# When a weight is converted: fewer conversion steps ahead of the last two layers, earlier low parts, a subtraction in two halves

## The chip, the cores and the metric

The kernel runs on one core of a Trainium2 chip. The core has TensorE (PE in the rows; its weight loads are PEld), VectorE (DVE), ScalarE (ACT), GpSimd (POOL) and SyncE (SP), which here only issues transfers. Each engine works through a queue of its own, strictly in order, and waits at an instruction until what it reads or overwrites is free. The metric is the device time of one execution in microseconds (us).

## The reference, cut to what matters

Three blocks in a row: attention with pooled keys and values (4 x 8 heads, 576 positions), a mixture of 8 experts over its 2304 tokens of 512 numbers, and a dense pair of layers. The change lies in the last one:

```
h = x @ w_in              # x: tokens x 512, w_in: 512 x 2048
r = np.maximum(h, 0.0)
g = s * (r * r) + b
return (g @ w_out)        # w_out: 2048 x 512
```

The weights w_in and w_out come as 64-bit floats. Tokens that an expert had no room for are zero at this point and all give the same row.

## The kernel before

**Numbers as high and low parts.** TensorE is given every operand twice: a high part (the value rounded by a cast, `w1h`, `yhl`, `gh`) and a low part (the value less the high part, `w1l`, `y1l`, `gl`). A product is three matmuls: high x high, high x low, low x high.

**The last layers** (`last_layers`) take the kept tokens in units of 256 (`CU`). Layer 1 makes the 2048 hidden numbers in 16 blocks `f` of 128 (`KF2`); one block is 12 matmuls of 256 columns (`layer1_y`, line 1040) into one PSUM bank. The block is then squared (`square`): ACT writes relu to `rt` (line 1424), DVE multiplies (line 1425); ACT casts the result to the high part `gh` (`parts`, line 1439) and POOL subtracts to get the low part `gl` (line 1440). Of every third block (`inside`, `f % 3 == 2`) DVE leaves the square in the PSUM bank and makes the low part itself; that bank is free only after this. Layer 2 is 6 matmuls of 512 columns per block (`layer2`, line 1445): two halves of the tokens, three products each.

**w_out.** It is loaded by SP in 16 pieces of 128 rows (line 1471) and rebuilt from its 64-bit pattern by `Weights64.step`: four steps a piece, each one or two DVE instructions (lines 871 to 883). The step after next then makes the high part (ACT, line 1399; for the first three pieces POOL, line 1397) and the low part (DVE, line 1400), and one adds the piece to a sum of rows in `raw3` (DVE, line 1405). `conv(n, end)` issues the next n steps. All this stands in the DVE queue between the squares.

**Units 0 and 1 go as a pair** (`pair`), because w_out isn't ready when they begin: layer 1 of unit 0, all 16 blocks (`first(0, 0, 16)`; the first four of them, `EARLY`, were multiplied at the end of the experts); layer 1 of unit 1, blocks 0 to 6 (`HEAD` = 7); layer 2 of both units for blocks 0 to 6 (`second`); layer 1 of unit 1, blocks 7 to 15; layer 2 of both for blocks 7 to 15. Unit 0's first layer goes round 8 PSUM banks, unit 1's round 4 (`ph`), while the other 4 (`po`) hold the sums of layer 2. Pieces 14 and 15 of w_out are loaded only after the first part of layer 2, into space that held parts of unit 1 till then. The tokens of unit 1 (`yr`) are loaded by SP behind piece 5; their high and low parts (`split_y`: ACT line 1032, DVE line 1033) are needed by unit 1's first block.

**Then come single units** (`unit`, four of them here), with POOL and DVE as above and nothing of w_out left to convert, **and at the end a unit of 128 tokens** (`half`): its first layer uses the sum of w_in's two parts as a single-precision weight, which DVE and POOL rebuild by turns, three blocks ahead (`whole`, line 1557), and its `gl` subtractions (128 columns) are POOL's as well.

The order is written out by hand: each engine's queue is the order of the calls below.

Of the kernel before, what the change touches and what calls it, by code (L numbers as in the profile page):

```python
# [33 lines left out]
KD = DM // P  # L34
# [541 lines left out]
HEAD = 7  # L576
# [793 lines left out]
def last_layers(nc, tc, c, a, pool, side, x, ps, out):  # L1370
# [13 lines left out]
    FIRST = len(x.c_raw)  # L1384
# [29 lines left out]
    def conv(n, end=len(steps)):  # L1414
        for _ in range(n):
            if done[0] < end:
                z, i = steps[done[0]]
                z.step(i)
                done[0] += 1

    def square(f, p, n, inside=False):

        r = rt[f % 4][:, :n]
        nc.scalar.activation(r, p, AF.Relu)  # L1424
        nc.vector.scalar_tensor_tensor(out=p if inside else r, in0=p, scalar=0.0, in1=r, op0=ALU.max, op1=ALU.mult)  # L1425

    def place(f, u=0):

        if u != 1 or HEAD <= f < KF2 - 2:
            f -= HEAD if u == 1 else 0  # L1430
            return gh[:, f], gl[:, f]
        t = spare[f % (KF2 - 2)] if f < 3 or f > HEAD else more[(f - 3) // 2][:, (f - 3) % 2]
        return t[:, 0], t[:, 1]

    def parts(f, n=CU, u=0, p=None):

        h, l = place(f, u)
        r = rt[f % 4][:, :n] if p is None else p
        nc.scalar.copy(h[:, :n], r)  # L1439
        (nc.gpsimd if p is None else nc.vector).tensor_sub(l[:, :n], r, h[:, :n])  # L1440

    def layer2(p, j, f, c=slice(0, DM), u=0):
        h, l = place(f, u)
        for i, (g, z) in enumerate(((h, 0), (h, 1), (l, 0))):
            nc.tensor.matmul(p[:, c], lhsT=g[:, j * P:j * P + P], rhs=wo[f][:, z, c], start=f == 0 and i == 0, stop=f == KF2 - 1 and i == 2)  # L1445
# [12 lines left out]
    def tokens(u):  # L1458
        if u < NV:
            for k in range(KD):  # L1460
                x.split_y(u, k, nc.gpsimd)
# [8 lines left out]
    def load_out(i):  # L1470
        nc.sync.dma_start(out=wo[i].rearrange("p c two -> p (c two)"), in_=wout[:, i])

    def pair():

        for i in range(KF2 - 2):
            load_out(i)
            if i == 5:
                x.load_y(1)
                for j, n in enumerate(("moe2_s", "moe2_b")):
                    nc.sync.dma_start(out=sb[:, j:j + 1], in_=a[n].unsqueeze(0).to_broadcast([P, 1]))  # L1480
        more.extend(side.tile([P, 2, 2, CU], F32R, name=f"wo{i}") for i in range(KF2 - 2, KF2))
        spare.extend(x.w.tile([P, 2, CU], F32R, name=f"raw{i}") for i in range(3))
        held = []

        def first(u, f0, f1, banks):
            for n, f in enumerate(range(f0, f1)):
                p = banks[f % len(banks)][:, :CU]
                if u or f >= EARLY:
                    x.layer1_y(u, p, *win[f])
                inside = f % 3 == 2  # L1490
                square(f, p, CU, inside)
                conv(1, steps_of_first)
                if u == 0 and 10 <= f < 10 + KD:
                    x.split_y(1, f - 10, nc.vector)
                if held:
                    parts(*held.pop())
                held.append((f, CU, u, p if inside else None))
            parts(*held.pop())

        def second(u, f0, f1, end):  # L1500
            for f in range(f0, f1):
                for j in range(2):
                    layer2(po[2 * u + j], j, f, u=u)
                conv(2, end)

        steps_of_first, all_steps = cvs[0].total, len(steps)
        conv(4 * FIRST)
        nc.gpsimd.memset(onesf, 1.0)
        first(0, 0, KF2, ps)
        first(1, 0, HEAD, ph)  # L1510
        x.load_y(2)
        second(0, 0, HEAD, steps_of_first)
        second(1, 0, HEAD, steps_of_first)
        for i in range(KF2 - 2, KF2):
            wo[i] = place_out(i, [P, DM, 2], I32)
            load_out(i)
        first(1, HEAD, KF2, ph)
        conv(all_steps, steps_of_first)
        second(0, HEAD, KF2, all_steps)
        tokens(2)  # L1520
        second(1, HEAD, KF2, all_steps)
        conv(all_steps)
        raw[0:3] = [x.w.tile([P, DM], F32, name=f"raw{i}") for i in range(3)]
        slots.extend(raw[2:4] + [x.w.tile([P, DM], F32, name="c_f1")])
        sums["drop"] = x.w.tile([P, DM], F32, name="c_u0")

    def unit(u):
        if u == 2:
            pair()
        if u + 1 < NV:  # L1530
            x.load_y(u + 1)
        for f in range(KF2):
            p = ph[f % 4][:, :CU]
            x.layer1_y(u, p, *win[f])
            square(f, p, CU)
            if f:
                parts(f - 1)
            if u == 2:
                if f == 1:
                    rows(ph[(f + 3) % 4])  # L1540
                elif f > 11:
                    store((f - 12) // 2, f % 2, po[f - 12])
        parts(KF2 - 1)
        tokens(u + 1)
        if u == 2:
            for f in range(len(slots)):
                whole(f)
        for j in range(2):
            p = po[2 * (u % 2) + j]
            for f in range(KF2):  # L1550
                layer2(p, j, f)
            store(u, j, p)
# [95 lines left out]
```

## Time and profile before

| | us |
|---|---|
| median of 3 runs | 648.42 (647.5 to 651.75) |
| the profiled execution | 649.79 |
| its span in the trace | 648.1 |
| PE busy | 588.7 (91%) |
| DVE busy | 367.0 (57%) |
| POOL busy | 267.8 (41%) |
| granted TensorE clock, mean | 0.959 |

The trace is of one execution; its times count from the start of the span, and the 1.7 us between span and execution lie around it. The last layers take from about 324 us to the end: the pair to 427 us, four single units to about 606 us, the half unit after that. A row of a timeline merges instructions of one kind that follow each other; in brackets stands how long the engine sat idle before, and what ended that.

### The profile page before, as it was taken

What the parts mean: (1) busy time and instruction counts of PE and PEld (TensorE: products, weight loads), DVE (VectorE), ACT (ScalarE), POOL (GpSimd) and SP (SyncE); (2) the same over time, 40 slices, a digit from 0 to 9 for tenths busy, and PEclk for the clock granted to TensorE, in tenths of its full rate; (3) what the DMA queues carried; (4) which work ended last, traced back from release to release, by engine and by line L of the source; (5) the groups of instructions that cost most, each with busy time, mean ns of one, the idle gap of its engine ahead of it and who ended that gap; (6) DMA issues with size and microseconds to landing.
All of it is one profiled execution on the core that took longest, in us unless ns stands there. A gap on an engine that the chain in (4) does not pass through costs nothing. (4 is left out here: it accounts for less than half of the span.)

```text
span 648.1 us, 11186 instructions
## 1 busy us (share of the span) xinstructions
PE 588.7 (91%) x4005; PEld 545.1 (84%) x4005; DVE 367.0 (57%) x893; ACT 249.9 (39%) x614; POOL 267.8 (41%) x384
## 2 busy tenths in 40 slices
PE   5887988799899979998887899999999999999894
PEld 5787877689799969997887889899899898898784
DVE  4687898888969956654499996424122021120140
ACT  1354554546356635533327425125034042141130
POOL 6557634627165717013234402216435054153381
PEclk8799999799899979999998799999999999999898
DMA  8999776637649884856565101135200101000000
GB/s 164 190 190 182 157 228 182 220 117 261 230 148 307 267 299 126 281 172 214 188 208 231 34 30 37 32 118 209 81 18 6 46 17 33 32 3 17 20 2 20
DMA packets 67950, 86.11 MB, mean 133 GB/s; under 512 B 24713, under 2 KB 40073, under 8 KB 67856
## 3 DMA queue, kind: packets, MB, share of 16 engines
q1 hardware_dynamic: 57168, 71.04, 37.2%
q10 hardware_dynamic: 8240, 7.14, 3.8%
q0 software_dynamic: 2448, 6.82, 3.3%
q8 instruction: 42, 0.69, 0.5%
q14 instruction: 52, 0.43, 0.2%
HBM read 68.09 MB, written 17.58 MB: 132 GB/s over the span
## 5 line engine op out<-in xcount | busy, mean ns | idle before, releaser
L1440 POOL TENSOR_TENSOR gl<-rt,gh 128x256 fp32r<-128x256 f32 (+1 forms) x96 | 71.3, 747 | 99.3 <-ACT gh L1439 57.9
L1445 PE MATMUL bank<-wo,gh 128*128 128x512 f32 (+1 forms) x340 | 99.2, 376 | 0.0
L1113 PE MATMUL bank<-hs,w2h 128*128 128x288 f32 (+1 forms) x308 | 68.9, 312 | 5.0 <-issue 4.6
L936 POOL TENSOR_TENSOR w1l<-kraw,w1h 128x128 fp32r<-128x128 f32 x96 | 51.9, 572 | 51.1 <-ACT w1h L929 51.1
L1445 PEld LDWEIGHTS bank<-wo,gh 128*128 128x128 f32 x340 | 62.0, 188 | 12.2
L1445 PE MATMUL bank<-wo,gl 128*128 128x512 f32 (+1 forms) x170 | 63.8, 375 | 0.0
L1452 DVE SCALAR_TENSOR_TENSOR raw<-bank,sb,c_u 128x512 f32<-128x512 f32 (+1 forms) x14 | 9.9, 710 | 86.9 <-PE bank L1445 86.9
L1113 PEld LDWEIGHTS bank<-hs,w2h 128*128 128x128 f32 x308 | 51.0, 193 | 6.0 <-issue 5.4
L1424 ACT ACTIVATE rt<-tq 128x256 f32<-128x256 f32 (+1 forms) x26 | 9.5, 367 | 113.8 <-PE tq L1040 91.1
L1113 PE MATMUL bank<-hs,w2l 128*128 128x288 f32 (+1 forms) x148 | 45.0, 304 | 0.0
L1425 DVE SCALAR_TENSOR_TENSOR rt<-bank,rt 128x256 f32<-128x256 f32 (+1 forms) x53 | 21.3, 401 | 37.6 <-ACT rt L1424 37.2
L944 POOL DMA_INDIRECT xg<-xd,u_idx x23 | 26.1, 1136 | 34.4 <-DVE r L290 15.3
L1439 ACT CAST gh<-rt 128x256 fp32r<-128x256 f32 (+1 forms) x96 | 36.6, 381 | 7.9 <-DVE rt L1425 7.9
L1453 POOL DMA_INDIRECT out_dram<-raw,it x12 | 11.9, 994 | 64.3 <-DVE raw L1452 63.8
L1445 PEld LDWEIGHTS bank<-wo,gl 128*128 128x128 f32 x170 | 31.9, 188 | 6.5
L1424 ACT ACTIVATE rt<-bank 128x256 f32<-128x256 f32 (+1 forms) x60 | 22.2, 369 | 33.7 <-PE bank L1040 26.5
L230 PE MATMUL sc<-kbd,qT 128*128 128x144 f32 (+1 forms) x152 | 25.5, 317 | 6.2 <-DVE rmine L380 3.6
L1425 DVE SCALAR_TENSOR_TENSOR rt<-tq,rt 128x256 f32<-128x256 f32 (+1 forms) x24 | 9.6, 399 | 35.5 <-ACT rt L1424 35.5
L967 PE MATMUL bank<-xs,w1h 128*128 128x288 f32 (+1 forms) x120 | 27.3, 313 | 2.0 <-DVE hs L970 2.0
L230 PEld LDWEIGHTS sc<-kbd,qT 128*128 128x128 f32 (+1 forms) x152 | 21.9, 201 | 8.4 <-issue 4.9
L1113 PEld LDWEIGHTS bank<-hs,w2l 128*128 128x128 f32 x148 | 28.5, 193 | 0.0
L940 DVE TENSOR_TENSOR w2l<-vraw,w2h 128x512 fp32r<-128x512 f32 x39 | 26.8, 686 | 0.9 <-ACT w2h L939 0.5
(496 smaller groups left out, 1749.4 us busy)
## 6 DMA issues: line engine op xcount, KB each, us to landing
kraw<-in_moe_w_dram SPq DMA_DIRECT2D x14, 1024.0 KB
vraw<-in_moe_w_dram SPq DMA_DIRECT2D x14, 1024.0 KB
c_raw<-in_moe_w_in_dram ACTq DMA_DIRECT2D x13, 512.0 KB
wo<-in_moe_w_out_dram SPq DMA_DIRECT2D x13, 512.0 KB
kraw<-in_k_dram SPq DMA_DIRECT2D x8, 576.0 KB
out_dram<-c_u SPq DMA_DIRECT2D x1, 4608.0 KB
q<-in_q_dram SPq DMA_DIRECT2D x16, 256.0 KB
xd<-xr SPq DMA_DIRECT2D x16, 256.0 KB
```

The lines of the kernel that those rows point to most:

```text
L230: nc.tensor.matmul(sc[:n, p // 2, p % 2 * 144:p % 2 * 144 + 144], lhsT=q[:, p, :n], rhs=kbd[b % 2][:, p], start=True, stop=True)
L936: eng.tensor_sub(self.w1l[:, i, z], self.w1(i)[:, z], self.w1h[:, i, z])
L940: eng.tensor_sub(self.w2l[i], self.w2r[:, i], self.w2h[i])
L944: self.nc.gpsimd.indirect_dma_start(out=dst, out_offset=None, in_=self.xd[:have], in_offset=bass.IndirectOffsetOnAxis(ap=idx[:n], axis=0), ...
L967: self.nc.tensor.matmul(p, lhsT=l[:, f, k], rhs=r[k], start=n == 0, stop=n == 3 * KD - 1)
L1113: nc.tensor.matmul(py[d][:, :v.n], lhsT=l[f][:, d * P:d * P + P], rhs=r[f], start=f == 0 and i == 0, stop=f == KF - 1 and i == 2)
L1424: nc.scalar.activation(r, p, AF.Relu)
L1425: nc.vector.scalar_tensor_tensor(out=p if inside else r, in0=p, scalar=0.0, in1=r, op0=ALU.max, op1=ALU.mult)
L1439: nc.scalar.copy(h[:, :n], r)
L1440: (nc.gpsimd if p is None else nc.vector).tensor_sub(l[:, :n], r, h[:, :n])
L1445: nc.tensor.matmul(p[:, c], lhsT=g[:, j * P:j * P + P], rhs=wo[f][:, z, c], start=f == 0 and i == 0, stop=f == KF2 - 1 and i == 2)
L1453: i = nc.gpsimd.indirect_dma_start(out=dst, out_offset=bass.IndirectOffsetOnAxis(ap=ids, axis=0), in_=o[:, c], in_offset=None, bounds_chec ...
```

## The change

Four edits in the last layers. (1) Ahead of the first square 6 conversion steps are issued instead of 12 (`conv(2 * FIRST)`), in unit 0's blocks 6 to 15 only every second block issues one, and the steps left over follow later: one instead of two after each block of unit 1's first part of layer 2, and one or two in each of unit 1's blocks 7 to 15, which had none. (2) Unit 1's tokens are split at blocks 7 to 10 of unit 0 instead of 10 to 13. (3) `conv(all_steps, steps_of_first)` ahead of the second part of layer 2 goes, since nothing is left for it. (4) POOL's `gl` subtraction is issued as two halves, in every unit.

```diff
         h, l = place(f, u)
         r = rt[f % 4][:, :n] if p is None else p
         nc.scalar.copy(h[:, :n], r)
-        (nc.gpsimd if p is None else nc.vector).tensor_sub(l[:, :n], r, h[:, :n])
+        if p is None:
+            for z in (slice(0, n // 2), slice(n // 2, n)):
+                nc.gpsimd.tensor_sub(l[:, z], r[:, z], h[:, z])
+        else:
+            nc.vector.tensor_sub(l[:, :n], r, h[:, :n])
...
                 square(f, p, CU, inside)
-                conv(1, steps_of_first)
-                if u == 0 and 10 <= f < 10 + KD:
-                    x.split_y(1, f - 10, nc.vector)
+                conv(f < 6 or f % 2 if u == 0 else 1 if f < HEAD else 1 + f % 2, steps_of_first)
+                if u == 0 and 7 <= f < 7 + KD:
+                    x.split_y(1, f - 7, nc.vector)
...
                     layer2(po[2 * u + j], j, f, u=u)
-                conv(2, end)
+                conv(1 if u and f < HEAD else 2, end)
...
         steps_of_first, all_steps = cvs[0].total, len(steps)
-        conv(4 * FIRST)
+        conv(2 * FIRST)
...
         first(1, HEAD, KF2, ph)
-        conv(all_steps, steps_of_first)
         second(0, HEAD, KF2, all_steps)
```

DVE's queue where unit 0's squares begin (`c_f`: a piece being rebuilt, `c_raw2` and `wo3`: raw pieces 2 and 3, `rt` and `bank2 <- ...`: squares of blocks 0, 1, 2). Before:

```order
L1400 TENSOR_TENSOR c_raw1_17124<-c_f1_17064,c_raw1_17124 128x512
L879 SCALAR_TENSOR_TENSOR c_f0_17063<-c_raw2_17081,c_f0_17063 128x512
L1405 TENSOR_TENSOR raw3_1963<-raw3_1963,c_f1_17064 128x512
L883 SCALAR_TENSOR_TENSOR c_f0_17063<-c_u0_17065,c_f0_17063 128x512
L1425 SCALAR_TENSOR_TENSOR rt0_1968<-tq_1607,rt0_1968 128x256
L871 TENSOR_SCALAR c_f1_17064<-wo3_17080 128x512
L1425 SCALAR_TENSOR_TENSOR rt1_1969<-misc_1608,rt1_1969 128x256
```

and now, from the square of block 3 on:

```order
L871 TENSOR_SCALAR c_f0_17063<-c_raw2_17081 128x512
L1425 SCALAR_TENSOR_TENSOR rt3_1971<-bank3_1943,rt3_1971 128x256
L874 TENSOR_SCALAR c_u0_17065<-c_raw2_17081 128x512
L877 SCALAR_TENSOR_TENSOR c_f0_17063<-c_raw2_17081,c_f0_17063 128x512
L1400 TENSOR_TENSOR c_raw1_17139<-c_f1_17064,c_raw1_17139 128x512
L1444 TENSOR_TENSOR gl_17067<-bank2_1942,gh_17066 128x256
```

Piece 2 was finished ahead of the square of block 0; now four squares have gone by when its first step is issued, and piece 1's low part comes behind the square of block 3.

DVE's queue where unit 1's blocks 7 to 15 begin (`rt3 <- bank3` is block 7's square, `tq <- tq` block 8's). Before:

```order
L1400 TENSOR_TENSOR wo13_17632<-c_f1_17064,wo13_17632 128x512
L1405 TENSOR_TENSOR raw3_1963<-raw3_1963,c_f1_17064 128x512
L1425 SCALAR_TENSOR_TENSOR rt3_1971<-bank3_1943,rt3_1971 128x256
L1425 SCALAR_TENSOR_TENSOR tq_1607<-tq_1607,rt0_1968 128x256
L1425 SCALAR_TENSOR_TENSOR rt1_1969<-misc_1608,rt1_1969 128x256
L1440 TENSOR_TENSOR gl_17067<-tq_1607,gh_17066 128x256
L1425 SCALAR_TENSOR_TENSOR rt2_1970<-bank2_1942,rt2_1970 128x256
```

and now:

```order
L871 TENSOR_SCALAR c_f1_17064<-wo11_17072 128x512
L1425 SCALAR_TENSOR_TENSOR rt3_1971<-bank3_1943,rt3_1971 128x256
L877 SCALAR_TENSOR_TENSOR c_f1_17064<-wo11_17072,c_f1_17064 128x512
L1400 TENSOR_TENSOR wo10_17654<-c_f0_17063,wo10_17654 128x512
L879 SCALAR_TENSOR_TENSOR c_f1_17064<-wo11_17072,c_f1_17064 128x512
L1405 TENSOR_TENSOR raw3_1963<-raw3_1963,c_f0_17063 128x512
L1425 SCALAR_TENSOR_TENSOR tq_1607<-tq_1607,rt0_1968 128x256
L883 SCALAR_TENSOR_TENSOR c_f1_17064<-c_u0_17065,c_f1_17064 128x512
L1425 SCALAR_TENSOR_TENSOR rt1_1969<-misc_1608,rt1_1969 128x256
L871 TENSOR_SCALAR c_f0_17063<-wo12_17071 128x512
L877 SCALAR_TENSOR_TENSOR c_f0_17063<-wo12_17071,c_f0_17063 128x512
L1400 TENSOR_TENSOR wo11_17694<-c_f1_17064,wo11_17694 128x512
```

All 14 pieces of the first load stood converted ahead of block 7's square; now piece 11 has just been begun there, and 14 steps stand among the nine squares.

POOL's queue in the half unit (`raw`, `c_f`: rebuilt single-precision weights). Before:

```order
L1557 TENSOR_TENSOR raw2_17932<-w2h0_146,w2l0_147 128x512
L1440 TENSOR_TENSOR gl_17067<-rt1_1969,gh_17066 128x128
L1440 TENSOR_TENSOR gl_17067<-rt2_1970,gh_17066 128x128
L1557 TENSOR_TENSOR c_f1_17933<-w2h_1951,w2l_1952 128x512
L1440 TENSOR_TENSOR gl_17067<-rt3_1971,gh_17066 128x128
```

and now:

```order
L1560 TENSOR_TENSOR raw2_17954<-w2h0_146,w2l0_147 128x512
L1442 TENSOR_TENSOR gl_17067<-rt1_1969,gh_17066 128x64 x2
L1442 TENSOR_TENSOR gl_17067<-rt2_1970,gh_17066 128x64 x2
L1560 TENSOR_TENSOR c_f1_17955<-w2h_1951,w2l_1952 128x512
L1442 TENSOR_TENSOR gl_17067<-rt3_1971,gh_17066 128x64 x2
```

Between two weights that POOL rebuilds stand four subtractions of 64 columns instead of two of 128.

## Rows read from the trace of the kernel before

**Rows 1.** Page, part 1: engine, busy us (share of the span), instructions.

```profile
PE 588.7 (91%) x4005; PEld 545.1 (84%) x4005; DVE 367.0 (57%) x893; ACT 249.9 (39%) x614; POOL 267.8 (41%) x384
```

**Rows 2.** Windows of 5 us: busy PE, PEld, DVE, ACT, POOL; granted clock, DMA share, GB/s.

```profile
335.00:340.00 5.00, 3.42 (x27) 3.02 (x26) 5.00 (x9) 2.49 (x7) 2.50 (x3) 1.00 0.51 165
340.00:345.00 5.00, 3.06 (x17) 3.06 (x18) 5.00 (x12) 3.04 (x10) 1.65 (x2) 0.77 1.02 412
...
350.00:355.00 5.00, 3.70 (x28) 3.09 (x26) 5.00 (x12) 3.34 (x10) 1.91 (x2) 1.00 0.02 7
355.00:360.00 5.00, 2.37 (x11) 2.16 (x12) 5.00 (x10) 1.68 (x6) 2.41 (x2) 0.63 0.09 8
```

**Rows 3.** Waits, 285 to 430 us: who waited for whom, us, times, longest.

```profile
PE tq L1040 <- DVE y1l L1033: 3.9, 4, 2.6
PE bank L1040 <- DVE gl L1440: 2.9, 1, 2.9
```

**Rows 4.** DVE's timeline: start, duration, line, operation; first step, first square, last y1l.

```profile
324.62 0.43 DVE L871 TENSOR_SCALAR c_f<-c_raw 128x512 int32<-128x512 int32 x1 [1.60 <-DMA c_raw<-in_moe_w_out_dram]
...
335.49 0.41 DVE L1425 SCALAR_TENSOR_TENSOR rt<-tq,rt 128x256 f32<-128x256 f32 x1
...
357.24 0.94 DVE L1033 TENSOR_TENSOR y1l<-yr,y1h 128x256 fp32r<-128x256 f32 x1
```

**Rows 5.** ACT's timeline: the relu of unit 0's block 0.

```profile
325.85 0.39 ACT L1424 ACTIVATE rt<-tq 128x256 f32<-128x256 f32 x1 [1.10 <-PE tq L1040]
```

**Rows 6.** PE's timeline: the first matmuls of layer 2.

```profile
369.29 0.63 PE L1445 MATMUL bank<-c_raw,gh 128*128 128x512 f32 x2
```

**Rows 7.** Chain of waits, in order of time: start, us, engine and line.

```profile
402.16 24.99 PE bank L1445 x108
...
433.57 1.41 PE tq L1040 x12
...
450.69 22.20 PE bank L1445 x96
```

**Rows 8.** DVE's timeline within layer 2: a piece's first step, an add, the next piece.

```profile
373.45 0.41 DVE L871 TENSOR_SCALAR c_f<-wo 128x512 int32<-128x512 int32 x1
...
376.04 0.68 DVE L1405 TENSOR_TENSOR raw<-raw,c_f 128x512 f32<-128x512 f32 x1
...
377.24 0.42 DVE L871 TENSOR_SCALAR c_f<-wo 128x512 int32<-128x512 int32 x1
```

**Rows 9.** DVE's timeline: an add beside POOL, block 7's square, the last low part.

```profile
371.37 1.23 DVE L1405 TENSOR_TENSOR raw<-raw,c_f 128x512 f32<-128x512 f32 x1
...
394.45 0.42 DVE L1425 SCALAR_TENSOR_TENSOR rt<-bank,rt 128x256 f32<-128x256 f32 x1
...
411.03 0.69 DVE L1400 TENSOR_TENSOR wo<-c_f,wo 128x512 fp32r<-128x512 f32 x1 [0.80 <-issue]
```

**Rows 10.** SP's timeline: the loads of unit 0's and unit 1's tokens.

```profile
317.21 0.42 SPq L1027 DMA_DIRECT2D yr<-yt  x1
...
332.33 0.46 SPq L1027 DMA_DIRECT2D yr<-yt  x1
```

**Rows 11.** ACT's timeline: the high parts of unit 0's tokens.

```profile
321.15 1.32 ACT L1032 CAST yhl<-yr 128x256 fp32r<-128x256 f32 x4 [3.35 <-DMA yr<-yt]
```

**Rows 12.** POOL's timeline: a subtraction of 256 columns; then the half unit.

```profile
432.95 0.73 POOL L1440 TENSOR_TENSOR gl<-rt,gh 128x256 fp32r<-128x256 f32 x1 [1.42 <-ACT gh L1439]
...
611.85 0.45 POOL L1440 TENSOR_TENSOR gl<-rt,gh 128x128 fp32r<-128x128 f32 x1
612.26 1.26 POOL L1557 TENSOR_TENSOR c_f<-w1h,w1l 128x512 f32<-128x512 f32 x1
```

**Rows 13.** A window of the half unit between two weights that POOL rebuilds.

```profile
620.60:623.10 2.50, 2.05 (x18) 1.86 (x17) 1.64 (x3) 0.93 (x4) 2.50 (x5) 1.00 0.00 0
```

**Rows 14.** Groups by line and shape, POOL: its small subtraction of the attention part.

```profile
L160 POOL TENSOR_TENSOR kp<-kraw 72x64 f32<-72x64 f32 x3 | 1.7, 552 | 0.2
```

**Rows 15.** PE's timeline in the half unit: block 15's matmuls.

```profile
626.92 1.16 PE L1565 MATMUL bank<-yr,raw 128*128 128x128 f32 x8 [0.45 <-POOL raw L1557]
```

## The prediction

> **What bounds the kernel now.** The page's busy shares [rows 1] say that PE works for 91% of the span. So time can be won only where PE waits, and I looked for that in the stretch that the change touches, the pair of units 0 and 1. Windows of 5 us came first [rows 2]: between 335 and 360 us PE is busy for 3.42, 3.06, 3.70 and 2.37 of 5 us, while DVE is busy for 5.00 in every one. The granted clock falls to 0.77 and 0.63 there, that is, TensorE spends part of these windows at 1.2 instead of 2.4 GHz, after PE has stood still. The waits [rows 3] name DVE both times: PE stands for the low part of a block that is made in its PSUM bank (2.9 us in one piece), and for the low parts of unit 1's tokens (3.9 us, 4 times). So DVE bounds this stretch, and DVE's timeline [rows 4] shows why: its first conversion step begins at 324.62, its first square at 335.49, though ACT had the relu of that block at 325.85 [rows 5]. Twelve steps stand between.
>
> How much is there to win? One block of layer 1 takes PE 1.41 us, one of layer 2 22.20/16 = 1.39 us [rows 7]. From 325.85, with block 0 done, 22 blocks remain to the first layer 2: 325.85 + 22 x 1.41 = 356.9. It begins at 369.29 [rows 6]. So 12.4 us are lost, to waits and to the low clock, and that is the ceiling.
>
> **The steps, counted.** The pair issues 70 steps before and now; only the places differ.
>
> | stretch | before | now |
> |---|---|---|
> | ahead of the first square | 12 | 6 |
> | unit 0, layer 1 | 16 | 11 |
> | unit 1, blocks 0 to 6 | 7 | 7 |
> | layer 2, first part, unit 0 / unit 1 | 14 / 10 | 14 / 7 |
> | unit 1, blocks 7 to 15 | 0 | 14 |
> | layer 2, second part | 11 | 11 |
>
> *Price of a step.* In a run of steps alone a piece (four steps) takes 377.24 - 373.45 = 3.79 us [rows 8], 0.95 a step, with waits for ACT's cast in it. The 12 at the start took 10.87 us [rows 4], 0.91 each; three of those hold one instruction more. Taking those out at about 0.34 us of queue time gives 0.82; I use 0.85 for a step between squares, where other work fills the waits.
>
> **Gain ahead of the first layer 2.** Eleven steps fewer stand on DVE's path: 11 x 0.91 = 10.0 us, and since DVE has no idle time in these windows, all of it counts. Layer 2 would begin at 359.3, still 2.4 us behind what PE alone could do; the ceiling leaves room. The earlier split of unit 1's tokens changes no sum of work, but takes DVE's last low part (now at 357.24, [rows 4]) from just ahead of unit 1's first block to well before it. It needs the tokens: their load is issued at 332.33; unit 0's took from 317.21 to 321.15, 3.9 us [rows 10, 11], so they land at about 336.3. Block 7 is done on PE at 325.85 + 7 x 1.41 = 335.7. ACT may wait for about 0.6 us there, with its next relus behind it; PE has eight banks at that point, so I cost it at nothing. Should the load take twice as long, ACT would stand for 4.5 us, and those banks (11 us of matmuls) still cover it.
>
> **What is given back later.** (a) *Piece 6.* When layer 2 begins, 24 steps are issued, and piece 6 needs six more and its low part. DVE comes to them about 2 us after PE's start, behind the last square and one step: 359.3 + 2 + 6 x 0.95 + 0.6 = 367.6. PE wants it after six blocks, at 359.3 + 6 x 1.39 = 367.6. A tie; I put in 0.8 us (0 to 2). The first part of layer 2 then ends at 359.3 + 14 x 1.39 + 0.8 = 379.5. (b) *Blocks 7 to 15.* DVE has done its 21 steps at 361.3 + 21 x 0.95 = 381.3, behind PE, which has only four banks. Block 15 needs the bank of block 11, whose low part comes behind nine of the 14 steps, six squares and two low parts (0.34 us each): 381.3 + 7.7 + 2.7 + 0.4 = 392.1, or 393 at 0.95 a step. PE alone would be there at 379.5 + 8 x 1.41 = 390.8. I take 2.0 us; none if DVE comes at its best, and 5.6 us if all of DVE's lateness (14 x 0.85 + 12 x 0.34 + 1.8 us behind, against PE's 12.7) falls on PE. So this ends at 379.5 + 12.7 + 2.0 = 394.2. (c) *Pieces 14 and 15*, the last nine steps: DVE's squares are over at 381.3 + 11.9 + 4.1 = 397.3, so piece 15 is ready at 397.3 + 8.6 = 405.9. PE wants it eight blocks after 394.2, at 405.3: 0.6 us (before it was there at 411.7, [rows 9], and wanted at 402.16 + 11.1 = 413.3). Their loads are issued 16 us before DVE reaches them. The call that the change drops ahead of the second part has no step left to issue.
>
> The pair then ends at 394.2 + 24.99 [rows 7] + 0.6 = 419.8, against 402.16 + 24.99 = 427.15 now: **7.3 us less**.
>
> **What the halved subtraction costs.** In the full units POOL's subtraction takes 0.73 us of a block's 1.41 [rows 12]; with another 0.15 it still hides. In the half unit it doesn't: POOL is busy for 2.50 of 2.50 us between two weights that it rebuilds, and PE, busy for 2.05, waits [rows 13]; its last block stands for POOL's weight too [rows 15]. From 256 to 128 columns the subtraction falls from 0.73 to 0.45 us, 0.0022 us a column, so 64 columns take 0.31, and two of them 0.62 instead of 0.45: 0.17 more, or 0.13 counted from start to start (612.26 - 611.85 = 0.41, [rows 12]). I take 0.15; ten of the 16 blocks lie ahead of the last weight: **1.5 us more**. The bounds: nothing, if DVE's turns fill the same time; and 10 x (2 x 0.552 - 0.45) = 6.5 us by the one POOL subtraction of 64 columns in the trace [rows 14], though that one ran beside DVE's work.
> The Trainium skill, GPSIMD Engine Reference, section 3.1 (Elementwise), speaks against this edit: an instruction passes two hops of software dispatch on GpSimd, where VectorE has one and pays about 156 ns. By that figure as a floor, ten more instructions would cost at least an estimated 1.6 us; the slope in the rows agrees.
>
> **Sum.** 649.79 - 7.3 + 1.5 = 644.0 us for an execution like the profiled one. That one stands 1.4 above the median of the three runs, from which the same change gives 642.6. Forecast: **643.5 us**.
>
> **The rivals.**
> 1. *More.* DVE gets through blocks 7 to 15 in time and (a) to (c) vanish. For it: adds that took 0.68 us alone took 1.23 beside POOL [rows 8, 9], and a POOL subtraction in two pieces lets DVE in sooner: at a wait of up to 0.3 us less for some ten such meetings, 3 us come back to DVE, about what (a) to (c) cost. Against it: four pieces now meet DVE where two did. Pair 10.7 us, net 9.2: 640.6, or 639.2 from the median.
> The Trainium skill, SBUF - State Buffer, section "Who interferes with whom", has the rule behind those rows: a VectorE instruction with two SBUF inputs and a GpSimd one that reads SBUF exclude each other for the whole instruction. By that rule shorter POOL instructions mean shorter waits; the 1.23 against 0.68 us agrees.
> 2. *Slower.* The debt is not paid in time: pieces 14 and 15 are converted so late that PE stands at the end of layer 2. Its place is DVE's queue among unit 1's squares, with 21 steps in it (7 and 14) and POOL's subtractions beside them, now two to a block. It decides from 5.8/21 = 0.28 us more per step, 1.13 instead of 0.85. For it: an instruction that meets POOL took 1.23 [rows 9], and that at every step gives 21 x 0.38 = 8.0 us, 652.0, or 650.6 from the median. Against it: before, DVE met POOL only now and then, and 12 steps in a row cost 0.91.
> 3. *The half unit eats it.* POOL's pieces cost the 0.55 us of rows 14: 649.79 - 7.3 + 6.5 = 649.0.
> 4. *The clock.* The waits of (b), about 2 us, let the granted clock fall once more, as after the 2.9 us wait [rows 2, 3]. A window of 5 us at 0.63 holds 3.7 us at the lower level, which cost half of that in work: 1.8 us more, 645.8.
>
> **Chances.** Forecast 0.56 (with its own bounds 641 to 647), more 0.23, slower 0.07, half unit 0.08, clock 0.06. The range reaches to the outer bounds of the forecast and to most of rivals 1, 3 and 4: 639.8 to 648.5, which leaves out rival 2 and the ends of 1 and 3. A measurement of this kernel can tell about 1%, 6.5 us: faster by more than that means 641.9 or less, which is most of rival 1 and the low end of the forecast, 0.30; slower by more, the far end of rival 2, 0.03; within, 0.67.
>
> **What the next profile would show.** DVE's first square at about 330; PE busy for 5 of 5 us and the clock at 1.00 from 335 to 355; the first matmul of layer 2 near 359; then, new, PE waits on line 1444 in blocks 12 and 15 and a short one for piece 15. In the half unit a longer period than 2.50 us with POOL still full. I would be wrong if layer 2 begins later than 362 (then something other than DVE's steps held it), if PE stands long for wo's low parts, or if the half unit grows by over 3 us.

## The result, and the profile after

The changed kernel takes **643.46 us** (median of 20 runs, 639.92 to 648.4), the kernel before, run by turns with it on the same chip, 649.47 us (20 runs, 644.6 to 656.05). The ratio on record, formed from the single executions without the few slow ones, is 0.9905, with a 95% interval of 0.9883 to 0.9928, so 0.95% less; the medians lie 6.0 us apart. The forecast was 643.5 us.

The profiled execution of the change took 640.99 us (span 639.2, mean granted clock 0.968), 2.5 us less than its median. So the two profiles lie 8.8 us apart and the medians 6.0; the profiles are read for where the time goes, the medians for how much it is.

Busy time on the page, beside [rows 1]; PE does the same 4005 matmuls in less busy time, and POOL has 102 instructions more:

```profile
PE 582.6 (91%) x4005; PEld 539.6 (84%) x4005; DVE 367.0 (57%) x893; ACT 250.0 (39%) x614; POOL 289.3 (45%) x486
```

Windows of 5 us, columns as in [rows 2], first ahead of layer 2, then in unit 1's blocks 7 to 15:

```profile
335.00:340.00 5.00, 5.00 (x46) 5.00 (x45) 4.73 (x11) 2.34 (x9) 3.61 (x6) 1.00 0.60 189
340.00:345.00 5.00, 5.00 (x44) 5.00 (x44) 4.49 (x10) 3.26 (x11) 4.57 (x7) 1.00 1.01 409
...
350.00:355.00 5.00, 5.00 (x45) 5.00 (x44) 4.94 (x11) 3.63 (x10) 4.07 (x8) 1.00 0.07 21
355.00:360.00 5.00, 3.46 (x23) 2.99 (x22) 5.00 (x11) 3.41 (x9) 3.72 (x6) 1.00 0.00 2
...
385.00:390.00 5.00, 3.19 (x28) 2.99 (x27) 4.96 (x11) 3.10 (x8) 2.88 (x4) 1.00 0.00 0
390.00:395.00 5.00, 4.17 (x32) 3.79 (x32) 5.00 (x9) 3.11 (x8) 2.65 (x5) 1.00 0.00 2
```

Up to 355 us PE is busy throughout, and the granted clock, which fell to 0.77 and 0.63 in [rows 2], stays at 1.00. Where PE is less busy now (355 to 360, 385 to 395), DVE is full. The waits of PE from 320 to 432 us (columns as in [rows 3]) and their places in PE's timeline:

```profile
PE tq L1040 <- DVE gl L1444: 1.8, 1, 1.8
PE bank L1040 <- DVE raw L1444: 1.5, 1, 1.5
PE bank L1040 <- DVE gl L1444: 0.8, 1, 0.8
PE bank L1449 <- DVE wo L1400: 0.4, 2, 0.2
```

```profile
356.89 0.39 PE L1040 MATMUL bank<-y1h,w1h 128*128 128x256 f32 x1 [1.54 <-DVE raw L1444]
...
358.44 0.63 PE L1449 MATMUL bank<-c_raw,gh 128*128 128x512 f32 x2
...
367.37 0.50 PE L1449 MATMUL bank<-wo,gh 128*128 128x512 f32 x1 [0.20 <-DVE wo L1400]
...
387.31 0.39 PE L1040 MATMUL tq<-y1h,w2h 128*128 128x256 f32 x1 [1.81 <-DVE gl L1444]
...
392.51 0.39 PE L1040 MATMUL bank<-y1h,w2h 128*128 128x256 f32 x1 [0.82 <-DVE gl L1444]
...
405.66 0.50 PE L1449 MATMUL bank<-wo,gh 128*128 128x512 f32 x1 [0.17 <-DVE wo L1400]
```

In order: unit 1's block 6, which waits for the bank of its block 2; the first matmul of layer 2; piece 6; blocks 12 and 15, which wait for the banks of blocks 8 and 11; piece 15. All but the first are waits that the prediction named. DVE's timeline, beside [rows 4, 9]: first step, first square, last low part of unit 1's tokens, low parts of blocks 8 and 11, last low part of w_out.

```profile
323.92 0.43 DVE L871 TENSOR_SCALAR c_f<-c_raw 128x512 int32<-128x512 int32 x1 [0.91 <-DMA c_raw<-in_moe_w_out_dram]
...
328.95 0.41 DVE L1425 SCALAR_TENSOR_TENSOR rt<-tq,rt 128x256 f32<-128x256 f32 x1
...
345.43 0.41 DVE L1033 TENSOR_TENSOR y1l<-yr,y1h 128x256 fp32r<-128x256 f32 x1
...
386.84 0.42 DVE L1444 TENSOR_TENSOR gl<-tq,gh 128x256 fp32r<-128x256 f32 x1
...
392.05 0.41 DVE L1444 TENSOR_TENSOR gl<-bank,gh 128x256 fp32r<-128x256 f32 x1
...
404.91 0.69 DVE L1400 TENSOR_TENSOR wo<-c_f,wo 128x512 fp32r<-128x512 f32 x1 [0.74 <-ACT wo L1399]
```

PE goes on 0.46 to 0.47 us behind the start of either of those low parts. POOL's timeline in the half unit, beside [rows 12]:

```profile
613.43 1.26 POOL L1560 TENSOR_TENSOR c_f<-w2h,w2l 128x512 f32<-128x512 f32 x1
614.65 1.60 POOL L1442 TENSOR_TENSOR gl<-rt,gh 128x64 fp32r<-128x64 f32 x4
616.21 1.26 POOL L1560 TENSOR_TENSOR raw<-w2h,w2l 128x512 f32<-128x512 f32 x1
```

From one rebuilt weight to the next pass 616.21 - 613.43 = 2.78 us, where 2.50 passed in [rows 13]: 0.28 for two more instructions, 0.14 each.

Five marks divide the last layers of every profile: DVE's first step; the first matmul of layer 2; the first matmul of unit 2 (until there is **the pair**); DVE's last store of a full unit; the first matmul of block 15 in the half unit (between these two is **half**). **End** is the time from DVE's last store to the end of the span. DVE's first step waits for a transfer and comes 0.70 to 2.16 us ahead of ACT's relu of unit 0's block 0, from which the prediction counts; so the first two columns can differ by up to 1.5 us for that alone, and a third gives the pair from that relu. All in us:

| kernel | to layer 2 | pair | pair from the relu | half | end | ratio on record |
|---|---|---|---|---|---|---|
| before | 44.67 | 102.37 | 101.14 | 20.34 | 8.68 | 1 |
| the change | 34.52 | 95.52 | 93.46 | 21.28 | 6.39 | 0.9905 |
| subtraction whole again | 34.50 | 96.76 | 96.00 | 19.59 | 8.51 | 0.9946 |
| halves in full units only | 34.98 | 96.00 | 94.43 | 20.49 | 6.65 | 0.9889 |
| tokens late again | 36.18 | 97.00 | 94.84 | 21.04 | 6.32 | 0.9882 |
| steps alone | 37.95 | 99.94 | 98.66 | 19.50 | 8.71 | 0.9913 |
| tokens alone | 43.88 | 101.17 | 99.86 | 20.21 | 8.42 | 0.9989 |
| halves alone | 43.18 | 100.42 | 98.93 | 21.17 | 6.75 | 0.9959 |
| 22 additions late | 33.57 | 91.55 | 90.26 | 20.33 | 7.50 | 0.9825 |
| 18 additions late | 36.00 | 94.54 | 92.69 | 19.47 | 6.36 | 0.9805 |
| before, 51 memsets | 44.46 | 101.97 | 100.65 | 18.40 | 6.98 | 0.9947 |
| before, 102 memsets | 44.74 | 102.66 | 101.11 | 20.49 | 8.53 | 0.9997 |
| before, 128 memsets | 44.58 | 102.17 | 101.47 | 20.44 | 8.42 | 1.0 |

The full units between pair and half took 179.6 us in each but one (22 additions late: 180.59). From before to the change the pair is 6.85 us shorter (7.68 from the relu) and half 0.94 longer: 5.9 us (6.7), beside the 6.0 of the medians. The end is 2.3 us shorter besides, and the last experiments are about that. Each kernel below was run 5 to 12 times, by turns with the kernel before on one chip, and not all on the same one; so their ratios are compared and not their times. The expectations were written with marks that give the pair about 0.15 us more.

### The profile page after: what moved, and what is told of

Read it like the earlier page. It is cut to its first block, busy times and chain, and to the rows that moved or that the text cites. A ratio compares the mean times of both kernels' runs of the same rounds, so it can differ in the third digit from the quotient of the medians.

```text
span 639.2 us, 11276 instructions
## 1 busy us (share of the span) xinstructions
PE 582.6 (91%) x4005; PEld 539.6 (84%) x4005; DVE 367.0 (57%) x893; ACT 250.0 (39%) x614; POOL 289.3 (45%) x486
## 5 line engine op out<-in xcount | busy, mean ns | idle before, releaser
L1442 POOL TENSOR_TENSOR gl<-rt,gh 128x128 fp32r<-128x128 f32 (+1 forms) x192 | 89.3, 488 | 77.6 <-ACT gh L1439 77.4
```

What stands on the lines that cost most here:

```text
L1442: nc.gpsimd.tensor_sub(l[:, z], r[:, z], h[:, z])
```

## The experiments

The theory was that of the prediction: DVE's steps and additions set when PE goes on, the halves help DVE and cost POOL in the half unit. The rivals: the halves or the earlier tokens do most of it, or the time is lost elsewhere.

### One part undone at a time

**The subtraction whole again:**

```diff
-        if p is None:
-            for z in (slice(0, n // 2), slice(n // 2, n)):
-                nc.gpsimd.tensor_sub(l[:, z], r[:, z], h[:, z])
-        else:
-            nc.vector.tensor_sub(l[:, :n], r, h[:, :n])
+        (nc.gpsimd if p is None else nc.vector).tensor_sub(l[:, :n], r, h[:, :n])
```

> The change with POOL's subtraction in one piece again. Measured in the trace: the pair from DVE's first conversion step of w_out to unit 2's first matmul (102.5 us before, 95.7 in the change), and the half unit from the last full unit's last store on DVE to the first matmul of block 15 (20.3 before, 21.3 in the change). Theory (DVE's amount of work sets the pair, the halves only let it in a little sooner): pair 96.3, half unit 20.4, the whole 0.3 us less than the change. Rival (the halves are what lets DVE through): pair 98.5 or more, the whole 2 us more than the change.

646.46 us, ratio 0.9946 (0.9914 to 0.9978). The pair is 1.24 us longer by the first step and 2.54 from the relu, half 1.7 shorter, the end 2.1 longer. The theory had 0.6 for the pair and the whole below the change; the ratio lies 0.4% above the change's (the intervals overlap). So the halves do more for the pair than the theory had, and the rival (2.8 for the pair, 2 us in the whole) is nearer, though part of the whole is the end. DVE's timeline shows what the halves do to it. An addition beside POOL, with the whole subtraction:

```profile
391.34 1.22 DVE L1405 TENSOR_TENSOR raw<-raw,c_f 128x512 f32<-128x512 f32 x1
```

and with the halves, in the change:

```profile
388.10 0.95 DVE L1405 TENSOR_TENSOR raw<-raw,c_f 128x512 f32<-128x512 f32 x1
```

Alone it takes 0.68 us [rows 8]. In these two profiles every addition of a piece takes 0.68 to 0.69 us, or 1.22 to 1.23 with the whole subtraction and 0.94 to 0.95 with the halves; one of 1.23 in the change is the last, beside unit 2's tokens, which POOL still splits whole. So a meeting costs 0.27 instead of 0.54 us: DVE gets in between the halves. The rule that the prediction weighed (the Trainium skill, SBUF - State Buffer, section "Who interferes with whom": two such instructions exclude each other as a whole) would have it so, and the trace agrees. PE's wait at block 6 and the clock behind it differ too (the kernel with the whole subtraction; PE's timeline, then a window):

```profile
358.92 0.39 PE L1040 MATMUL bank<-y1h,w1h 128*128 128x256 f32 x1 [2.27 <-DVE raw L1440]
```

```profile
360.00:365.00 5.00, 5.00 (x20) 4.11 (x18) 4.97 (x9) 2.30 (x5) 2.27 (x3) 0.66 0.00 0
```

A wait of 2.27 us, and the clock is at 0.66, so partly at 1.2 GHz; in the change the wait is 1.54 us, and the clock stays at 1.00. The length of the wait alone doesn't decide it, though: with the halves alone (further down) PE waited 2.68 us in unit 0's blocks, and the clock stayed at 1.00 (PE's timeline, then the window behind it):

```profile
347.70 0.50 PE L1040 MATMUL bank<-yhl,w2h 128*128 128x256 f32 x2 [2.68 <-DVE gl L1444]
```

```profile
350.00:355.00 5.00, 5.00 (x44) 4.96 (x43) 5.00 (x12) 3.26 (x10) 3.04 (x5) 1.00 1.03 415
```

**Halves in the full units only:**

```diff
-            for z in (slice(0, n // 2), slice(n // 2, n)):
+            for z in (slice(0, n // 2), slice(n // 2, n)) if n == CU else (slice(0, n),):
```

> The change with the subtraction in two halves only for blocks of 256 columns, in one piece in the half unit. Theory (in the half unit POOL is full, so ten more instructions cost 0.1 us each): pair 95.7, half unit 20.4, the whole 0.9 us less than the change. Rival (the half unit's extra time has nothing to do with POOL's instructions): half unit 21.3.

642.76 us, ratio 0.9889 (0.9858 to 0.9921). Half is 20.49 instead of 21.28 us, so the cost of the halves in the half unit, 0.8 us, comes back; the medians can't separate 0.7 us. The 19.59 us with the whole subtraction everywhere has a second reason, the clock. At the start of the half unit PE waits for a weight that POOL rebuilds, 2.3 to 2.8 us in every profile but that with 51 memsets. Behind this wait the clock fell in some profiles and not in others; the kernel before and the steps alone, which run the same half unit (a window, then PE's timeline, of each):

```profile
610.00:615.00 5.00, 3.06 (x16) 3.06 (x17) 1.84 (x5) 1.12 (x5) 4.30 (x5) 0.73 0.01 3
...
611.94 1.75 PE L1565 MATMUL bank<-yr,raw 128*128 128x128 f32 x8 [2.72 <-POOL raw L1557]
```

```profile
610.00:615.00 5.00, 4.69 (x42) 4.50 (x42) 2.65 (x6) 1.85 (x8) 5.00 (x7) 1.00 0.00 0
...
609.71 1.16 PE L1564 MATMUL bank<-yr,raw 128*128 128x128 f32 x8 [2.69 <-POOL raw L1556]
```

The same eight matmuls take 1.75 us at the fallen clock and 1.16 at 1.00. Where the clock stayed (whole again, steps alone, 18 additions late) half is 19.47 to 19.59 us, and where it fell, with the subtraction of 128 columns in one piece, 20.21 to 20.49. With halves it fell each time, and half is 21.04 to 21.28. So at a like clock the halves cost about 0.8 us there, and some 0.9 us is whether the clock falls.

**The tokens late again:**

```diff
-                if u == 0 and 7 <= f < 7 + KD:
-                    x.split_y(1, f - 7, nc.vector)
+                if u == 0 and 10 <= f < 10 + KD:
+                    x.split_y(1, f - 10, nc.vector)
```

> The change with unit 1's tokens split at blocks 10 to 13 of unit 0 again. Theory (DVE bounds the pair; a wait of PE for the tokens' low parts takes the place of waits that come later anyway): PE waits 1 to 3 us ahead of unit 1's first block, the wait at its block 6 (1.8 us) goes, pair 96.5 against 95.7. Rival (the earlier split is worth the whole wait of 3.9 us that it removed): pair 99.6.

642.37 us, ratio 0.9882 (0.984 to 0.9924). PE waits 2.0 us for the tokens' low parts, and the wait at block 6 (1.54 us; the expectation's 1.8 is block 12's) is gone: one wait takes the other's place. The pair is 1.5 us longer (1.4 from the relu); the median isn't, and the intervals overlap. So the earlier tokens, on top of the rest, are worth between nothing and 1.5 us.

### One part alone

**The steps alone** (both edits above undone):

> Of the change only the conversion steps' new places; tokens split at blocks 10 to 13, POOL's subtraction in one piece. Without the halves alone the pair took 96.9 us, without the earlier tokens alone 97.2, the change 95.7, the kernel before 102.5. Theory (both act through DVE's time and add up): pair 98.4, half unit about 20, the whole 4 us less than before. Rival (the two cover each other, either one is enough): pair 97.2.

645.14 us, ratio 0.9913 (0.9882 to 0.9944); the pair takes 99.94 us, 1.5 more than expected. Its waits and two of its windows say why:

```profile
PE tq L1040 <- DVE y1l L1033: 2.6, 2, 1.7
PE tq L1040 <- DVE gl L1440: 2.1, 1, 2.1
```

```profile
350.00:355.00 5.00, 3.25 (x16) 3.04 (x16) 4.87 (x11) 3.17 (x9) 2.34 (x3) 0.74 0.39 121
...
390.00:395.00 5.00, 2.91 (x18) 2.92 (x19) 4.97 (x10) 2.88 (x8) 1.57 (x2) 0.84 0.00 0
```

PE waits for the tokens, then for block 8's low part, and the clock falls both times, to 0.74 and 0.84, that is, part of these windows runs at 1.2 GHz. The ratio can't be told from the change's 0.9905, and with the earlier tokens added (the subtraction whole again) it is 0.9946, within the same intervals. So what the two other edits add to the steps is read from the profiles alone.

**The tokens alone, and the halves alone** (the kernel before with that one edit):

> Of the change only the earlier split of unit 1's tokens (blocks 7 to 10). Theory (DVE is full there, so the wait of 3.9 us for the tokens' low parts only turns into waits for squares behind it): pair 102.0 against 102.5. Rival (the wait itself was on the path): pair 98.6.

649.17 us, ratio 0.9989 (0.9961 to 1.0018): no difference that can be told, as expected; the pair is 1.2 us shorter, where 0.5 was expected.

> Of the change only POOL's subtraction in two halves. Theory (DVE, full until layer 2, is held for shorter at each meeting with POOL, worth 1.2 us in the pair; the half unit loses 1 us): pair 101.3, half unit 21.3, the whole as before. Rival (DVE now meets POOL twice in a block): pair 103 or more, the whole 2 us more.

647.5 us, ratio 0.9959 (0.9934 to 0.9985). Expected was 1.2 us in the pair and nothing in the whole. The pair is 1.95 us shorter and half 0.83 longer, which leaves 1.1; the end is 1.9 us shorter, so most of the gain in the whole may be the end's and not DVE's. PE still waits 2.7 us for a low part and 4.2 us for the tokens.

Alone the three edits shorten the pair by 2.43, 1.20 and 1.95 us, 5.6 together; in one kernel they take 6.85. That they help one another because together they shorten the waits behind which the clock fell fits the windows of the pair (0.74, 0.66 and 0.56 at the lowest with one edit, 1.00 throughout in the change); it was not shown by itself.

### Taking work out of the stretch

If DVE's amount of work makes the waits that are left, then they go when its additions to the sum of rows (line 1405) come later, behind the pair's last step. Halves stay in the full units only.

```diff
     def add(i, f):
+        if 3 <= i < KF2 - 2:
+            return
...
         second(1, HEAD, KF2, all_steps)
         conv(all_steps)
+        for i in range(3, KF2 - 2):
+            for z in range(2):
+                nc.vector.tensor_add(raw[3], raw[3], wo[i][:, z])
```

> The subtraction in halves only for 256 columns, and the sums of w_out's rows for pieces 3 to 13 (11 adds of 0.60 us in DVE's queue while it bounds the pair) taken later, from the two parts, behind the last conversion step, where DVE stands idle for 15 us: 22 adds. Theory (the waits of PE in blocks 6, 12, 15 and for piece 15 are DVE's amount of work): they go, pair 91, with 89.4 as PE's floor; half unit 20.4; the whole 5 us less than the change, 638. Rival (they come from where the low parts stand in the queue, not from the amount): pair 94 or more, the whole 2 us less.

639.92 us, ratio 0.9825 (0.9774 to 0.9876); the pair takes 91.55 us, 4.45 less than with the additions in their place. The theory (91) held against the rival (94 or more) for the pair; the whole came out 2 us above the 638 expected. A new wait came (PE's waits, then DVE's timeline):

```profile
PE tq L1472 <- DVE rt L1427: 1.1, 1, 1.1
PE bank L1040 <- DVE raw L1446: 0.8, 1, 0.8
PE tq L1040 <- DVE gl L1446: 0.6, 1, 0.6
```

```profile
404.63 17.20 DVE L1530 TENSOR_TENSOR raw<-raw,wo 128x512 f32<-128x512 f32 x22
421.75 0.42 DVE L1427 SCALAR_TENSOR_TENSOR rt<-tq,rt 128x256 f32<-128x256 f32 x1
```

Blocks 12 and 6 are left with 0.6 and 0.8 us of their waits. But the 22 additions, each on the sum of the last, take 17.20 us, and unit 2's first square stands behind them; that is the 1.0 us in the full units.

**Two pieces fewer late** (`KF2 - 4` in both places, 18 additions):

> As the kernel that takes the sums of pieces 3 to 13 late, but only pieces 3 to 11: 18 late adds, which took 0.72 us each there, 13.0 us instead of 15.9. Theory (22 adds end at 421.8 and hold unit 2's first squares, for which PE waits 1.1 us): this wait goes, the adds of pieces 12 and 13 cost DVE 1.2 us among unit 1's last squares, of which PE sees 0.5; the whole 0.6 us less than with 22 late adds. Rival (every add that DVE does in the pair costs PE its whole time): no difference or 0.5 us more.

**638.52 us**, ratio 0.9805 (0.9775 to 0.9834): 1.95% below the kernel before, and the fastest of all here by its median. Its additions take 14.30 us and are over ahead of unit 2's square, so the full units take 179.60 us again. In this profile the pair is 3 us longer than with 22 (2.4 from the relu), where 0.5 was expected; ACT's timeline has part of the reason:

```profile
334.32 0.41 ACT L1441 CAST gh<-rt 128x256 fp32r<-128x256 f32 x1 [6.21 <-DMA yt<-yo]
```

The first cast waited 6.21 us for a transfer (4.32 with 22 additions, 3.63 in the change), and PE then stood for 0.99. Both kernels issue the same up to there, so I take the difference for one from run to run. Against the halves in full units only, this profile has the pair 1.5 us shorter and half 1.0, the latter by the clock that stayed at 1.00; how much of the 0.84% between the two ratios the moved additions make is open. In this profile the cast is what is late next.

### The end of the execution

The end takes 8.4 to 8.7 us in the four profiles of kernels with whole subtractions and 6.3 to 7.5 in the six others, at whichever place the halves were. That can't be what DVE or PE wait for, since all that is behind it is the last store. Where the instructions lie might be: the trace has packets of instructions that land in that stretch. So POOL got instructions that do nothing useful (102, 128 and 51 of them) in the kernel before, where it stands idle:

```diff
         first(1, 0, HEAD, ph)
         x.load_y(2)
+        for _ in range(102):
+            nc.gpsimd.memset(onesf[:, 0:1], 1.0)
```

> The kernel before, with 102 memsets of one column each on POOL behind unit 1's block 6, where POOL stands idle for 23.4 us in the kernel before; nothing else is changed. This is for the end of the execution. From DVE's last store to the end of the span pass 8.4 to 8.7 us in the four profiles without halved subtractions (before 8.68) and 6.3 to 7.5 in the six with them (the change 6.39); in the first four a last instruction packet lands about 1.4 us behind the last data of the store, in the others the last instruction packet comes ahead of it. Theory: it is the number of POOL's instructions alone, which decides where the last piece of code falls. Then the pair stays at 102.4 us, and the stretch from DVE's last store to the end is 6.4 us; the whole is 2 us shorter than before. Rival: the halves themselves, or chance from run to run, make it; then the stretch is 8.4 to 8.7 here, and the whole as before.

650.39 us, ratio 0.9997 (0.9975 to 1.0019), end 8.53: as before, against the theory. POOL has as many instructions here as in the change.

> As the last one, with 128 memsets. Theory: the end of the code lies elsewhere again; if POOL's code comes in pieces of 128 instructions, 128 more bring the end back to where it was: 8.7 us from DVE's last store to the end, and the whole as before. Rival: as the one with 102, either way.

650.13 us, ratio 1.0 (0.9972 to 1.0027), end 8.42.

> As the last ones, with 51 memsets. Theory: between the two: the last piece of code begins about half a piece further back than in the kernel before, so that it is asked for ahead of the last store: 6.4 us from DVE's last store to the end, 2 us less in the whole. Rival (the halves): 8.4 to 8.7 us, the whole as before.

646.16 us, ratio 0.9947 (0.9923 to 0.997): with 51 instructions that do nothing the median is 4.3 us lower, and the ratio says 0.5%. The end takes 6.98 us, and half 18.40 instead of 20.34. POOL's and PE's timelines at the half unit's beginning, first before:

```profile
610.28 1.60 POOL L1557 TENSOR_TENSOR raw<-w1h,w1l 128x512 f32<-128x512 f32 x1 [1.70 <-issue]
...
611.94 1.75 PE L1565 MATMUL bank<-yr,raw 128*128 128x128 f32 x8 [2.72 <-POOL raw L1557]
```

and with 51 memsets:

```profile
611.34 1.28 POOL L1559 TENSOR_TENSOR raw<-w1h,w1l 128x512 f32<-128x512 f32 x1
...
612.68 1.16 PE L1567 MATMUL bank<-yr,raw 128*128 128x128 f32 x8 [0.72 <-POOL raw L1559]
```

Before, POOL waited 1.70 us for nothing that the profile shows ("issue"); with 51 more instructions ahead it goes on at once, and PE waits 2.0 us less. The clock stays at 1.00 behind that shorter wait, which is part of the 1.94 us too. The last 9.2 us of the span in 40 slices, GB/s in each, before and with 51 memsets:

```profile
GB/s 0 0 0 0 0 0 0 36 0 0 71 0 267 263 36 18 0 18 0 0 0 0 0 0 0 36 0 0 0 0 0 0 0 0 0 0 0 0 0 0
```

```profile
GB/s 0 0 0 71 0 0 0 0 0 0 0 0 0 0 36 0 0 0 71 178 321 67 0 0 18 0 0 18 0 0 0 0 0 0 0 0 0 0 0 0
```

Before, a packet lands by itself in slice 25 of 0 to 39, twelve slices (12 x 0.23 = 2.8 us) behind the store's bulk (267 and 263). At 36 GB/s for 0.23 us it holds 8 KB, the size of the instruction packets of one queue (0.43 MB in 52 on the page). With 51 memsets such a packet and a larger one (slices 14 and 3) land ahead of the store, and none so late. So it is in all thirteen profiles: in the six with an end of 8.4 to 8.7 us the last instruction packet begins 0.4 to 1.6 us behind the store's last data, in the seven others 0.7 to 1.9 us ahead of it. What is shown is that instructions on whose result nothing waits move two stretches by 1.7 and 1.9 us. That they do so by where a piece of the program's instructions begins and is loaded is my reading of these packets; it was not shown by itself, and the count that decides wasn't found. The shorter end can thus come without the halves' work; what makes it in the change stays open.

## Why the prediction was right

**Ahead of layer 2: the sum right, partly by luck.** Forecast 10.0 us less; from the first step to layer 2 pass 34.52 instead of 44.67 us, 10.15 less (from the relu 32.47 instead of 43.44, 10.97 less). PE alone could have been there 22 x 1.41 = 31.0 us behind block 0's relu, which is at 325.97: at 357.0. It came at 358.44, and the wait of 1.54 us at block 6 makes up the difference. That wait was not in the prediction, which left 2.4 us there without a place. But the prediction gave all 10.0 us to the steps, 11 x 0.91, and the steps alone bring 6.7 (37.95 instead of 44.67, and 6.8 from the relu). The other 3.4 come from the earlier tokens and the halves, without which PE waits for the tokens' low parts and the clock falls to 0.74. I had costed the tokens at nothing: put late again in the change, they delay layer 2 by 1.7 us, and with the subtraction whole besides by 3.4. So the argument that every step counts in full because DVE has no idle time was too strong, and an effect that the prediction left out made up for it.

**Given back: the sum right, the parts shifted.** (a) piece 6: 0.8 forecast, 0.2 measured. (b) blocks 12 and 15: 2.0 forecast, 1.8 + 0.8 = 2.6. (c) piece 15: 0.6 forecast, 0.2. The three make 3.0 of 3.4, and from layer 2 to unit 2 pass 61.00 instead of 57.70 us, 3.30 more. The pair is 6.85 us shorter, 7.68 from the relu; 7.3 was forecast. (The upper bound of (b) adds up to 5.1 us and not 5.6; nothing hangs on it.)

**The half unit: the mechanism right, the size too large.** 0.14 us for each more POOL instruction, where 0.15 was taken. Half is 0.94 us longer than before; 1.5 was forecast. Over the three profiles with halves there and the four without in which the clock fell as well (the memsets aside) it is 21.16 against 20.34, 0.8 us. Not each of the ten instructions, then, cost PE its full time.

**The rivals.** *More* was partly at work: the halves cost DVE 0.27 instead of 0.54 us at a meeting and are worth 1.2 us of the pair in the full change (2.5 from the relu), near the 3 of the rival, and the waits (b) did not vanish. *Slower* did not come: DVE's last low part is done at 404.91 + 0.69 = 405.60, where 405.9 was forecast; an addition that meets POOL took 0.95 us there and not the 1.23 on which this rival rests. *The half unit* grew by 0.94 us, not 6.5. *The clock* stayed at 1.00 in the change's pair; that some luck is in this is likely, since it fell to 0.66 behind 2.27 us of waiting with the whole subtraction and to 0.74 with the steps alone, but stayed behind 2.68 us with the halves alone.

**Not in the prediction:** the clock at the start of the half unit, which fell in the change (0.66 from 605 to 610 us) as it had before; and the end of the execution, 2.3 us shorter in the profile. Pair and half alone give 5.9 us, beside the 6.0 of the medians; with the end they give 8.2, near the 8.8 between the two profiled executions. How much of it the medians hold stays open. (The section on the change counts one square too many: by the order shown there, three squares and not four stand ahead of piece 2's first step.)

## What to carry to other kernels

Where two engines take turns at the same memory, count the meetings and their length: cutting the instruction of the engine with slack in two gave the other 0.27 us back at a meeting, and cost 0.14 us where the first engine had no slack. Work that nobody waits for soon, like the additions here, should leave the stretch before anything in it is reordered: moving 22 of them out made the pair 4.45 us shorter, and with 18 the ratio went from 0.9889 to 0.9805, not all of which need be the additions. Profiles should be compared at a like clock: in the half unit the clock alone made 0.9 us. And an effect under 1% from an edit that adds instructions needs controls with several numbers of instructions that do nothing: one with as many, 102, would have missed the 0.5% that 51 made.

## What was not expected of the hardware

- With 51 memsets of one column that nothing waits for the program's median was 4.3 us lower (ratio 0.9947), and 102 or 128 changed nothing (0.9997 and 1.0).
- PE's clock fell behind single waits of 2.27 us (to 0.66) and 2.1 us (to 0.84), and behind two close together that make 2.6 us (to 0.74); behind the change's waits of 1.54 and 1.81 us it stayed at 1.00. But it also stayed at 1.00 behind waits of 2.33 to 2.69 us (halves alone in the pair; whole again, steps alone and 18 additions late in the half unit). So a wait of over 2 us may or may not cost the clock, in the half unit even in the same code.
- In the half unit a rebuilding addition on DVE takes 1.48 us in the change and 1.23 before, where it takes 0.68 alone. It isn't the smaller pieces that hold it: POOL's own rebuild of 1.26 us runs when it begins (DVE's and POOL's timelines, before and then the change):

```profile
620.60 1.26 POOL L1557 TENSOR_TENSOR c_f<-w2h,w2l 128x512 f32<-128x512 f32 x1
621.18 1.23 DVE L1557 TENSOR_TENSOR raw<-w2h,w2l 128x512 f32<-128x512 f32 x1
```

```profile
613.43 1.26 POOL L1560 TENSOR_TENSOR c_f<-w2h,w2l 128x512 f32<-128x512 f32 x1
613.76 1.48 DVE L1560 TENSOR_TENSOR raw<-w2h,w2l 128x512 f32<-128x512 f32 x1
```

DVE's ends 0.55 us behind POOL's both times (622.41 and 621.86; 615.24 and 614.69); it only began earlier under it, 0.33 instead of 0.58 us behind POOL's start.
